# mLSTM cell and squared-ReLU FFN: another order of a step's transfers on the one issuing queue, and weight and block sums moved along VectorE's queue

## The chip, the core and the metric

The kernel runs on one core of one Trainium2 chip. The metric is device time in microseconds (us): the median of the timed runs. A core has a matrix engine (TensorE, PE in the profile, with PEld for its weight loads), VectorE (DVE), ScalarE (ACT), GpSimd (POOL), and a queue of SyncE (SPq) from which nearly all transfers of this kernel are issued, one after the other. The profile is that of one execution.

## The reference, cut to what matters

```python
# attention: batch 4, 8 heads, 768 positions, head size 40
for t in range(S):
    m_new  = np.maximum(f_gate[:, :, t] + m, i_gate[:, :, t])
    f_stab = np.exp(f_gate[:, :, t] + m - m_new)
    i_stab = np.exp(i_gate[:, :, t] - m_new)
    C = f_stab[..., None, None] * C + i_stab[..., None, None] * np.einsum('bhd,bhe->bhde', vt, kt)
    n = f_stab[..., None] * n + i_stab[..., None] * kt
    h_tilde = np.einsum('bhde,bhe->bhd', C, qt)
    denom = np.maximum(np.abs(np.einsum('bhd,bhd->bh', n, qt))[:, :, None], 1.0)
    y[:, :, t] = sigmoid(o_gate[:, :, t]) * h_tilde / denom
# bridge (B,H,S,D) -> (B*S, H*D) = (3072, 320), then
h = np.maximum(x @ w_in, 0.0)          # 320 -> 2048
out = (h * h) @ w_out                  # 2048 -> 320
```

The recurrence is computed in chunks of 128 positions: 24 chunks `s` (6 for each of 4 batch entries). Inside a chunk, the decay between two positions is `exp(A[t] + b[t'])`, where `A` is a running sum of gates for each head; between chunks a state `C` is carried.

## The kernel before: what the change touches

The main loop has *parts* `n`, four to a chunk: `s = 6 + n // 4`, `at = n % 4`. A part holds a quarter of one FFN product of a *group* `g` of two chunks, and beside it one piece of the attention of chunk `s` or `s + 1`. Every engine and the issuing queue work through their own instructions in the order in which the program emits them.

```python
parts = [(1, 2, i) for i in range(4)] + [(2, 0, i) for i in range(4)]
for g in range(1, NG):                                   # NG = 12 groups
    parts += [(2, g, i) for i in range(4)]               # second FFN product of group g: s even
    if g + 2 < NG:
        parts += [(1, g + 2, i) for i in range(4)]       # first FFN product of g + 2 ("fast"): s odd
for n, (which, g, i) in enumerate(parts):
    s, at = 6 + n // 4, n % 4
    ...
    even = s >= 8 and s % 2 == 0
    squares_soon = s >= 7 and s % 2 == 1
    fast = which == 1 and g > 2
    if at == 0:
        if s < 8 or even:
            do(score, s)                   # PE scores; DVE weights them (L458)
        if even:
            do(turn_kq, s + 1)             # DVE 32x32 transposes of the loaded squares (L325)
    if at == 1:
        if even:
            do(lambda s: scores(s, ("h", "h")), s + 1)   # PE, L436: needs turn_kq(s + 1)
        if fast:
            ffn1_rows(g, 0, True)          # PE, L862
        do(attend_turned, s)               # PE numT (L533, L542), dC; DVE transposes tn (L559)
        do(decays, s + 1)                  # ACT exp of the broadcast A (L378)
        do(mask, s + 1)                    # POOL (L368)
        ...
        do(store_num, s)                   # transfer: tn -> DRAM (L571)
        if squares_soon:
            do(load_squares, s + 2)        # 4 transfers of small pieces (L318)
            do(load_num, s)                # 4 transfers: numerators back, turned (L576)
        do(load, s + 4)                    # k and v of s + 4 (L305)
        if 8 <= s < 20:
            load_o(s + 4)                  # L333
        if not squares_soon:
            do(load_num, s)
        do(pair_up, s + 3)                 # 4 transfers DRAM to DRAM (L296)
    ...
    if which == 2 and 0 < g < NG - 1 and i == 3:
        sums(g + 1, slice(0, NPAIR), (2,))               # DVE, block sum S2 (L751)
    if which == 2 and g > 1 and i < 2:
        sums(g, slice(0, NPAIR), (3 + i,))
    if n in (10, 11):
        for more in range(2):
            sums_of_win(2 * (n - 10) + more)             # DVE, sums of w_in (L810, 812, 814, 816)
    ...
    if fast:
        if i % 2:
            ffn1_close(g, i // 2, i == 1)
            ...
        else:
            ffn1_open(g, i // 2)
        ...
    else:
        ffn2_fast(g, i)                    # (for g > 0)
    if at == 2:
        do(lambda s: weigh(s, masked=True), s + 1)       # ACT exp (L392)
        ...
        do(normalise_turned, s)            # DVE, begins at L588: needs load_num(s)
        do(store_rows, s)                  # L623
        if not squares_soon:
            do(load_squares, s + 2)
        do(load_rows, s)                   # L628, needs store_rows(s)
        do(load_A, s + 2)                  # one transfer: A broadcast to all partitions (L343)
```

What the pieces do that matter here:

```python
def load_A(s):                              # two buffers; A[s + 2] takes that of A[s]
    A = ld.tile([P, H, P], F32, name="A_bc", bufs=2)
    nc.sync.dma_start(A[:], bass.AP(A_d.tensor, ..., [[0, P], [S, H], [1, P]]))   # 512 KB

def store_num(s):                           # transposed numerators to DRAM, 256 KB
    nc.sync.dma_start(n_d[s], st[s]["tn"]...)

def load_num(s):                            # read back in another order, 4 x 64 KB
    for m in range(P // SQ):
        nc.sync.dma_start(N[m * SQ : (m + 1) * SQ]..., n_d[s, :, m * P : (m + 1) * P]...)

def load_squares(s):                        # k and q of a chunk as 32x32 squares
    for i in range(2):
        for e in range(0, D, SQ):           # 128 KB in runs of 128 bytes, 32 KB in runs of 32 bytes
            nc.sync.dma_start(t[DP * i + e : ...], kq_d[s, i, ...]...)

def ffn1_open(g, q):                        # first half of a fast first product
    X, Y, V, Z = st["f1"] = [ps_h.tile([P, 4, P], F32, name="h_ps") for _ in range(4)]
    blocks(X, F11, xT[:, 0, 0, :], q, True)          # PE, L830
    nc.scalar.copy(m1[:], X[:])                      # ACT, L843
    blocks(Y, WS[1], xs[:, 3, :], q, True)
    nc.vector.tensor_tensor(U2[:], Y[:], m1[:], op=ALU.add)     # DVE, L845
    blocks(V, WS[0], xs[:, 0, :], q, True)
    nc.vector.tensor_tensor(U4[:], V[:], U2[:], op=ALU.add)     # DVE, L847
    blocks(Z, F22, xs[:, 4, :], q, True)

def ffn1_close(g, q, begun):                # adds on into the same banks
    blocks(X, F12, xT[:, 0, 1, :], q, False)         # PE; X must have been copied (L843)
    ...
    nc.scalar.activation(g4[:, :, 0, t0], X[:], AF.Relu)        # ACT, L878
    tt(U2[:], U2[:], Y[:], op=ALU.add)               # DVE, L879 to L882
    ...
```

`ffn1_rows` adds on into X and Y, so it needs the copy of X (L843) and the addition that reads Y (L845). `sums_of_win` 0 and 1 give `WS[0]` and `WS[1]`; 2 overwrites F21 with F11 − F21; 3 gives `WS[3]` from `WS[1]`.

Of the kernel before, what the change touches and what calls it, by code (L numbers as in the profile page):

```python
# [29 lines left out]
def kernel(  # L30
# [38 lines left out]
    NPAIR = NF // 2  # L69
    GT = 2  # L70
    NG = NT // GT
# [255 lines left out]
    def load_o(s):  # L327
        b, c = divmod(s, NB)
        r, (s0, s1) = next((r, (a, z)) for r, (a, z) in enumerate(RUNS) if a <= s < z)
        if s == s0:  # L330
            st["og", r] = ld.tile([P, 4, H, D], F32, name="og")
        og = st.setdefault(s, {})["og"] = st["og", r][:, s - s0]
        nc.sync.dma_start(og, o_gate[b, :, c * P : (c + 1) * P, :].rearrange("h p d -> p h d"))  # L333
# [314 lines left out]
    def new_g2(g):  # L648
        if g < 2:
            st["g2", g] = ffn.tile([P, NF, WG], F32, name=f"g2_{g}", bufs=1)  # L650
        else:
            st["g2", g] = g2c if g == 2 else st["g2", g - 3]
# [152 lines left out]
    def sums_of_win(i):  # L805
        tt = nc.vector.tensor_tensor
        if i != 2:
            WS[i] = late.tile([P, NPAIR, P], F32, name=f"WS{i}", bufs=1)[:]
        if i == 0:
            tt(WS[0], F21, F22, op=ALU.add)  # L810
        elif i == 1:
            tt(WS[1], WS[0], F11, op=ALU.subtract)
        elif i == 2:
            tt(F21, F11, F21, op=ALU.subtract)
        else:
            tt(WS[3], F12, WS[1], op=ALU.subtract)
# [18 lines left out]
    def ffn1_open(g, q):  # L835
        if q == 0:
            new_g2(g)
        xT, xs = st["xT", g], st["xs"]
        X, Y, V, Z = st["f1"] = [ps_h.tile([P, 4, P], F32, name="h_ps") for _ in range(4)]
        m1, U2, U4 = [ffn.tile([P, 4, P], F32, name="r_sb", bufs=4) for _ in range(3)]  # L840
        st["U"] = U2, U4
        blocks(X, F11, xT[:, 0, 0, :], q, True)
        nc.scalar.copy(m1[:], X[:])  # L843
        blocks(Y, WS[1], xs[:, 3, :], q, True)
        nc.vector.tensor_tensor(U2[:], Y[:], m1[:], op=ALU.add)  # L845
        blocks(V, WS[0], xs[:, 0, :], q, True)
        nc.vector.tensor_tensor(U4[:], V[:], U2[:], op=ALU.add)  # L847
        blocks(Z, F22, xs[:, 4, :], q, True)
# [45 lines left out]
    def do(f, s):  # L894
        if 0 <= s < NT:
            f(s)
# [20 lines left out]
    def load_part(s, i):  # L917
        b, c = divmod(s, NB)
        dst, src = load_parts(s)[i]
        nc.sync.dma_start(dst, src[b, :, c * P : (c + 1) * P, :].rearrange("h p d -> p h d"))  # L920
# [64 lines left out]
    for u in range(8):  # L985
        s = 2 + u // 2
# [70 lines left out]
    for n, (which, g, i) in enumerate(parts):  # L1057
        s, at = 6 + n // 4, n % 4
        if n == 5:
            brought.close()  # L1060
            late = ctx.enter_context(tc.tile_pool(name="late", bufs=1, side="right"))
        even = s >= 8 and s % 2 == 0
        squares_soon = s >= 7 and s % 2 == 1
        fast = which == 1 and g > 2
        if at == 0:
            if s < 8 or even:
                do(score, s)
            if even:
                do(turn_kq, s + 1)
        if at == 1:  # L1070
            if even:
                do(lambda s: scores(s, ("h", "h")), s + 1)
            if fast:
                ffn1_rows(g, 0, True)
            do(attend_turned, s)
            do(decays, s + 1)
            do(mask, s + 1)
            if n > 4 and not even and not fast:
                do(turn_kq, s + 1)
            do(decay_C, s + 1)  # L1080
            if s > X_SQ and not fast:
                do(turn_squares, s - 1)
            do(store_num, s)
            if squares_soon:
                do(load_squares, s + 2)
                do(load_num, s)
            do(load, s + 4)
            if 8 <= s < 20:
                load_o(s + 4)
            if not squares_soon:  # L1090
                do(load_num, s)
            do(pair_up, s + 3)
        if 5 <= n < 8:
            sums_of_weights(n - 5)
        if n == 6:
            sums(1, slice(0, NPAIR), (1, 2))
        if n == 8:
            sums_of_weights(3)
            sums(1, slice(0, NPAIR), (3,))
        if n == 9:  # L1100
            sums(1, slice(0, NPAIR), (4,))
        if which == 2 and 0 < g < NG - 1 and i == 3:
            sums(g + 1, slice(0, NPAIR), (2,))
        if which == 2 and g > 1 and i < 2:
            sums(g, slice(0, NPAIR), (3 + i,))
        if n in (10, 11):
            for more in range(2):
                sums_of_win(2 * (n - 10) + more)
        if at == 3 and s >= 8 and s % 2 == 0 and s // 2 - 1 < NG:
            sums_of_x(s // 2 - 1)  # L1110
        if at == 2 and not fast:
            if n > 4:
                do(scale_q, s + 1)
        if at == 3:
            if s % 4 == 3:
                for r in range(s + 1, min(s + 5, NT)):
                    sigmoid(r)
# [4 lines that stand above are left out]
                    do(turn_kq, s + 1)  # L1122
                    do(turn_squares, s - 1)
            else:
                ffn1_open(g, i // 2)
            if at == 2:
                do(scale_q, s + 1)
        elif which == 1:
            ffn1_main(g, i)
            if i % 2 == 0:  # L1130
                held = st["half"]
            else:

                both = held, st["half"]
                for more, half in enumerate(both):
                    ffn1_rest(g, i - 1 + more, half[0])
                for half in both:
                    st["half"] = half
                    relu_half()
                    square_half()  # L1140
        elif g == 0:
            ffn2(g, *divmod(i, 2))
        else:
            ffn2_fast(g, i)
        if at == 2:
            do(lambda s: weigh(s, masked=True), s + 1)
            ffn1_square()
            if n < 4:
                do(turn_kq, s + 1)
                do(scale_q, s + 1)  # L1150
            if even:
                do(weighted, s + 1)
            do(normalise_turned, s)
            do(store_rows, s)
            if not squares_soon:
                do(load_squares, s + 2)
            do(load_rows, s)
            do(load_A, s + 2)
        if at == 0:
            ffn1_square()  # L1160
        if n < 5:
            while rounding.done < LAST[n]:
                rounding.step()
# [30 lines left out]
```

## Time and profile before

The median of three runs is 521.55 us (518.85 to 525.43). The profiled execution took 521.29 us, of which the profile's span is 519.5 us.

| Engine or queue | busy, us | share of the span |
|---|---|---|
| PE | 498.4 | 96% |
| PEld | 457.9 | 88% |
| VectorE | 339.0 | 65% |
| ScalarE | 248.3 | 48% |
| GpSimd | 109.0 | 21% |

| Transfer (all from SPq) | count | KB each | us to landing, median |
|---|---|---|---|
| A broadcast, `A_bc<-a_rows` | 22 | 512 | 4.7 |
| numerators out, `num_rows<-tn` | 18 | 256 | 3.5 |
| numerators back, `kq<-num_rows` | 72 | 64 | 2.5 |
| squares, `kqT<-kq_rows` | 34 + 34 | 128 and 32 | 3.3 and 3.0 |
| rows out and back, `x_rows`, `xT` | 18 and 72 | 192 and 48 | 2.1 and 2.5 |

How to read the profile's lines: the first two numbers of a timeline line are the start in us from the span's start and the duration in us of what the line merges; then the engine, the source line of the kernel, the operation, what is written and read, and the count. In brackets stands the idle time of that engine just before, and what ended it. A "landing" is the time from a transfer's issue until its completion is signalled. An engine's wait matters only if it makes PE wait, since PE is the busiest.

### The profile page before, as it was taken

The numbers are of one execution on the slowest core, as the hardware profiler recorded it, in microseconds if no ns is written. First come the engines' busy times: TensorE is split into PE (matmuls) and PEld (weight loads), VectorE is DVE, ScalarE is ACT, GpSimd is POOL, SyncE is SP. The second block draws the span as 40 slices with busy tenths as digits, with TensorE's granted clock in tenths as the row PEclk, the third lists the DMA queues.
The fourth block names the chain that finished last, engine by engine and source line by source line (L and its number), as shares of the span: only waits on it lengthen the run. The fifth ranks groups of instructions, "written<-read, shape, count | busy, mean of one in ns | idle before, by whom it ended". The sixth has DMA issues, their size and how long they took to land.

```text
span 519.5 us, 13523 instructions
## 1 busy us (share of the span) xinstructions
PE 498.4 (96%) x5497; PEld 457.9 (88%) x5497; DVE 339.0 (65%) x630; ACT 248.3 (48%) x492; POOL 109.0 (21%) x138
## 2 busy tenths in 40 slices
PE   9989999999998999989999999989899899999997
PEld 4867788787797999989999899979899899999997
DVE  8588966555876866576667766476676676644441
ACT  3768897564440650661642672542482462432500
POOL 3356743321040130112102103103103111020000
PEclk9999999999998999999999999999999999999999
DMA  9999999665645775875765756775754632200000
GB/s 191 226 211 231 234 232 228 104 128 100 163 108 117 146 141 94 169 167 96 165 150 111 162 140 122 147 170 107 160 133 99 137 96 56 80 13 27 1 27 25
DMA packets 238237, 67.73 MB, mean 130 GB/s; under 512 B 185600, under 2 KB 232704, under 8 KB 238176
## 3 DMA queue, kind: packets, MB, share of 16 engines
q1 hardware_dynamic: 238080, 66.68, 61.4%
q8 instruction: 43, 0.70, 0.6%
q10 hardware_dynamic: 96, 0.20, 0.1%
q14 instruction: 18, 0.15, 0.1%
HBM read 54.56 MB, written 17.86 MB: 139 GB/s over the span
## 4 chain that ended last, share of the span: by engine, by line
PE 69%; SPq 8%; DVE 8%; DMA 6%; issue 4%; ACT 3%; POOL 1%; DVEq 0%; POOLq 0%; ACTq 0%
PE h_ps L756 25%; PE h_ps L830 12%; PE h_ps L665 7%; PE h_ps L862 5%; SPq L318 4%; PE h_ps L702 3%; DMA A_bc<-a_rows 3%; PE numT L542 3%; SPq L628 2%; PE h_ps L676 2%; PE hp L481 2%; PE h_ps L436 1%; DVE A_bc L458 1%; PE tp L436 1%; PE idle L909 1%
## 5 line engine op out<-in xcount | busy, mean ns | idle before, releaser
L368 POOL TENSOR_SCALAR_AFFINE_SELECT A_bc<-A_bc 128x1024 f32<-128x1024 f32 x22 | 24.9, 1134 | 223.9 <-ACT kq L378 189.6
L378 ACT ACTIVATE kq<-A_bc 64x512 f32<-64x512 f32 x30 | 18.8, 628 | 80.2 <-DMA A_bc<-a_rows 80.0
L756 PE MATMUL h_ps<-T,S 128*128 128x160 f32 x352 | 51.5, 299 | 0.7 <-DVE g L880 0.7
L756 PEld LDWEIGHTS h_ps<-T,S 128*128 128x128 f32 x352 | 49.0, 190 | 0.9 <-PE h_ps L756 0.9
L392 ACT ACTIVATE A_bc<-A_bc,b_T 128x128 f32<-128x128 f32 x144 | 44.0, 388 | 11.2 <-POOL A_bc L368 10.8
L756 PE MATMUL h_ps<-w_out,g 128*128 128x160 f32 x336 | 49.2, 303 | 0.0
L756 PEld LDWEIGHTS h_ps<-w_out,g 128*128 128x128 f32 x336 | 46.1, 190 | 1.4 <-issue 1.2
L665 PE MATMUL h_ps<-xT,w_in 128*128 128x256 f32 x192 | 44.2, 383 | 2.2 <-ACT xT L644 1.6
L830 PE MATMUL h_ps<-xT,w_in 128*128 128x128 f32 x288 | 39.3, 280 | 4.9 <-ACT r_sb L843 4.9
L665 PEld LDWEIGHTS h_ps<-xT,w_in 128*128 128x128 f32 x192 | 35.5, 190 | 8.1 <-ACT xT L644 2.0
L830 PEld LDWEIGHTS h_ps<-xT,w_in 128*128 128x128 f32 x288 | 35.2, 191 | 6.6 <-ACT r_sb L843 5.7
L772 DVE TENSOR_TENSOR y_sb<-y_sb,h_ps 128x160 f32<-128x160 f32 x44 | 14.0, 318 | 40.7 <-PE h_ps L756 40.6
L559 DVE STREAM_TRANSPOSE tn<-numT 128x256 f32<-128x256 f32 x36 | 16.0, 450 | 37.3 <-PE numT L542 37.3
L862 PE MATMUL h_ps<-xT,w_in 64*64 64x128 f32 x864 | 37.2, 275 | 2.8 <-DVE r_sb L845 2.8
L830 PE MATMUL h_ps<-xs,w_in 128*128 128x128 f32 x288 | 38.0, 275 | 0.0
L843 ACT COPY r_sb<-h_ps 128x512 f32<-128x512 f32 x18 | 10.5, 584 | 55.8 <-PE h_ps L830 55.8
L862 PEld LDWEIGHTS h_ps<-xT,w_in 64*64 64x64 f32 x864 | 32.0, 133 | 5.7 <-DVE r_sb L845 3.5
L830 PE MATMUL h_ps<-xs,WS 128*128 128x128 f32 x288 | 35.1, 275 | 0.0
L830 PEld LDWEIGHTS h_ps<-xs,w_in 128*128 128x128 f32 x288 | 35.1, 192 | 0.0
L830 PEld LDWEIGHTS h_ps<-xs,WS 128*128 128x128 f32 x288 | 33.6, 192 | 0.0
L756 PE MATMUL h_ps<-w_out,g_c 128*128 128x160 f32 x192 | 28.0, 302 | 0.0
L756 PEld LDWEIGHTS h_ps<-w_out,g_c 128*128 128x128 f32 x192 | 26.3, 190 | 0.7 <-issue 0.5
(173 smaller groups left out, 1041.0 us busy)
## 6 DMA issues: line engine op xcount, KB each, us to landing
A_bc<-a_rows SPq DMA_DIRECT2D x22, 512.0 KB, 4.7
raw<-in_moe_w_out_dram SPq DMA_DIRECT2D x8, 640.0 KB, 4.6
num_rows<-tn SPq DMA_DIRECT2D x18, 256.0 KB, 3.5
kq<-num_rows SPq DMA_DIRECT2D x72, 64.0 KB, 2.5
kqT<-kq_rows SPq DMA_DIRECT2D x34, 128.0 KB, 3.3
raw<-in_moe_w_in_dram SPq DMA_DIRECT2D x8, 512.0 KB, 6.0
kq<-in_k_dram SPq DMA_DIRECT2D x24, 160.0 KB, 4.4
va<-in_v_dram SPq DMA_DIRECT2D x24, 160.0 KB, 4.7
```

The lines of the kernel that those rows point to most:

```text
L318: nc.sync.dma_start(t[DP * i + e : DP * i + e + SQ, :, :w], kq_d[s, i, :, :, :, e : e + w].rearrange("n j (m r) a -> r (n j m) a", r=SQ),)
L368: nc.gpsimd.affine_select(A[:], A[:], compare_op=ALU.is_ge, fill=-1e30, base=0, pattern=[[0, H], [1, P]], channel_multiplier=-1,)
L378: nc.scalar.activation(e[rows], st[s]["A"][0][rows, PR * i : PR * (i + 1), :], AF.Exp)
L392: nc.scalar.activation(d["W"][:, i * n + h, :], A[i][:, h, :], AF.Exp, bias=b_T[:, b, c, i * n + h : i * n + h + 1],)
L542: nc.tensor.matmul(numT[i][halves[g], e, :], lhsT=va_w[s % NKQ][:, h * D1 : h * D1 + DP], rhs=d["P"][h % 2][:, h // 2, :] if s < KQ_SQ els ...
L559: nc.vector.transpose(to[:, 2 * i : 2 * i + 2], numT[i][:, :2, :].rearrange("p c t -> p (c t)"))
L665: nc.tensor.matmul(hs[i][:, n, :], lhsT=w_in[:, a, fb * P : (fb + 1) * P], rhs=xT[:, :, a, :], start=(n == 0 and a == 0), stop=False,)
L702: nc.tensor.matmul(o_ps, lhsT=st["g2", g][:, fb, j * P : (j + 1) * P], rhs=w_out[:, fb, :], start=(fb == 0), stop=(fb == NF - 1),)
L756: nc.tensor.matmul(to, lhsT=lhsT[:, p], rhs=rhs[:, p, :], start=(start and p == 0), stop=(p == NPAIR - 1), skip_group_check=True,)
L772: add = lambda to, a, b: nc.vector.tensor_tensor(to, a, b, op=ALU.add)
L830: nc.tensor.matmul(to[:, n, :], lhsT=lhsT[:, 4 * q + n, :], rhs=rhs, start=(start and n == 0), stop=True, skip_group_check=True,)
L862: nc.tensor.matmul(to[cols, n, :], lhsT=w_in2[rows, 4 * q + n, cols], rhs=rhs, start=(start and n == 0), stop=True, skip_group_check=True,)
```

## The change

Four things move; no arithmetic is added or taken away.

1. From chunk 8 on, the broadcast of `A` for chunk `s + 2` is issued right behind the store of the numerators of `s`, at `at == 1`, and no longer at the end of `at == 2`.
2. From chunk 8 on, the order behind that store is the same for all chunks: A, k, the numerators' loads, then (odd chunks) the squares, then v, the o gate and the pairs. Before, odd chunks issued the squares ahead of the numerators' loads, and even chunks k, v and o.
3. The squares of chunk 9, issued at chunk 7, go from `at == 1` to `at == 2`.
4. On VectorE, block sum S2 of group `g + 1` moves from the last part of `ffn2_fast(g)` to the part behind, after the two additions of `ffn1_open`. The four sums of `w_in` move from parts 10, 10, 11, 11 to parts 9, 10, 10, 11.

It is for having the transfers on which engines wait land sooner, and for having the additions that release PE's banks not stand behind long sums on VectorE.

```diff
-        squares_soon = s >= 7 and s % 2 == 1
 ...
             do(store_num, s)
-            if squares_soon:
-                do(load_squares, s + 2)
+            if s >= 8:
+                do(load_A, s + 2)
+                do(lambda s: load_part(s, 0), s + 4)
                 do(load_num, s)
-            do(load, s + 4)
-            if 8 <= s < 20:
-                load_o(s + 4)
-            if not squares_soon:
+                if not even:
+                    do(load_squares, s + 2)
+                do(lambda s: load_part(s, 2), s + 4)
+                if s < 20:
+                    load_o(s + 4)
+            else:
+                do(load, s + 4)
                 do(load_num, s)
             do(pair_up, s + 3)
 ...
-        if which == 2 and 0 < g < NG - 1 and i == 3:
+        if which == 2 and i == 3 and g == NG - 2:
             sums(g + 1, slice(0, NPAIR), (2,))
         if which == 2 and g > 1 and i < 2:
             sums(g, slice(0, NPAIR), (3 + i,))
-        if n in (10, 11):
-            for more in range(2):
-                sums_of_win(2 * (n - 10) + more)
+        for more in {9: (0,), 10: (1, 2), 11: (3,)}.get(n, ()):
+            sums_of_win(more)
 ...
             else:
                 ffn1_open(g, i // 2)
+                if i == 0:
+                    sums(g - 1, slice(0, NPAIR), (2,))
 ...
             do(store_rows, s)
-            if not squares_soon:
+            if s < 8 or even:
                 do(load_squares, s + 2)
             do(load_rows, s)
-            do(load_A, s + 2)
+            if s < 8:
+                do(load_A, s + 2)
```

## The prediction, made before the changed kernel was run

> **What bounds the kernel now.** I read the table of engines first.
>
> ```profile
> PE 498.4 (96%) x5497; PEld 457.9 (88%) x5497; DVE 339.0 (65%) x630; ACT 248.3 (48%) x492; POOL 109.0 (21%) x138
> ```
>
> PE is the bound, and a change that touches no matmul can win back only idle PE time: 519.5 - 498.4 = 21.1 us. So I went through PE's timeline for every idle stretch. From chunk 8 on (about 144 us) there are eleven. The eight that matter:
>
> ```profile
> 163.74 1.12 PE L862 MATMUL h_ps<-xT,w_in 64*64 64x128 f32 x31 [2.43 <-DVE r_sb L845]
> 221.36 2.41 PE L756 MATMUL h_ps<-T,S 128*128 128x160 f32 x16 [0.72 <-DVE g L880]
> 224.86 0.46 PE L436 MATMUL h_ps<-kqT 40*64 40x128 f32 x5 [1.09 <-issue]
> 252.85 1.16 PE L830 MATMUL h_ps<-xT,w_in 128*128 128x128 f32 x8 [0.68 <-ACT r_sb L843]
> 292.85 1.16 PE L830 MATMUL h_ps<-xT,w_in 128*128 128x128 f32 x8 [1.17 <-ACT r_sb L843]
> 343.59 1.22 PE L436 MATMUL h_ps<-kqT 40*64 40x128 f32 x32 [2.50 <-issue]
> 372.48 1.16 PE L830 MATMUL h_ps<-xT,w_in 128*128 128x128 f32 x8 [1.57 <-ACT r_sb L843]
> 411.81 1.16 PE L830 MATMUL h_ps<-xT,w_in 128*128 128x128 f32 x8 [1.50 <-ACT r_sb L843]
> ```
>
> With three more (0.17 at 263.29, 0.21 at 281.49, 0.16 at 321.20) they make 12.20 us. The other 8.9 us lie where the change does nothing: 0.93 at the start, 4.96 in six gaps up to 97 us, 3.03 after PE's last product (516.47). The gaps have three causes.
>
> *First, late A.* The timeline of chunk 19, all engines, around the gap at 372.48:
>
> ```profile
> 365.56 0.42 SPq L343 DMA_DIRECT2D A_bc<-a_rows  x1
> 370.06 1.27 ACT L378 ACTIVATE kq<-A_bc 64x512 f32<-64x512 f32 x2 [11.34 <-DMA A_bc<-a_rows]
> 371.84 0.58 ACT L843 COPY r_sb<-h_ps 128x512 f32<-128x512 f32 x1
> ```
>
> ScalarE stands 11.34 us at `decays` for A; behind it queues the copy of X that lets PE go on. A was issued at 365.56 at the end of a queue. Chunks 13, 15, 19, 21 show this: 0.68 + 1.17 + 1.57 + 1.50 = 4.92 us.
>
> *Second, late numerators.* Chunk 17, around 343.59, where the page gives only "issue":
>
> ```profile
> 326.99 0.38 SPq L571 DMA_DIRECT2D num_rows<-tn  x1
> 327.43 4.69 SPq L318 DMA_DIRECT2D kqT<-kq_rows  x4
> 332.21 3.12 SPq L576 DMA_DIRECT2D kq<-num_rows  x4
> 336.95 0.17 DVE L588 TENSOR_SCALAR dm<-kq 128x8 f32<-128x8 f32 x1 [4.83 <-DMA kq<-num_rows]
> 342.25 1.23 DVE L325 STREAM_TRANSPOSE kqT<-kqT 128x1024 f32<-128x1024 f32 x1
> ```
>
> VectorE waits 4.83 us for numerators issued behind 4.69 us of squares; normalising, four additions, weighting and the transposes of the next squares follow in order, and PE's scores start at 343.59, just after that transpose ends (343.48). These gaps: 0.72 + 1.09 + 0.17 + 2.50 = 4.48 us.
>
> *Third, VectorE's queue ahead of the first opening:*
>
> ```profile
> 159.37 1.22 DVE L751 TENSOR_TENSOR S<-S,g_c 128x1024 f32<-128x1024 f32 x1
> 160.50 1.22 DVE L814 TENSOR_TENSOR w_in<-w_in 128x1024 f32<-128x1024 f32 x1
> 161.64 1.22 DVE L816 TENSOR_TENSOR WS<-w_in,WS 128x1024 f32<-128x1024 f32 x1
> 163.01 0.68 DVE L845 TENSOR_TENSOR r_sb<-h_ps,r_sb 128x512 f32<-128x512 f32 x1
> ```
>
> L845 ends at 163.69 and L862 starts at 163.74: 2.43 us, with 0.37 us more of the kind in chunks 15 and 17. It also cost clock. A table of stages, columns stretch, length, busy us (instructions) of PE, PEld, DVE, ACT and POOL, granted clock, DMA share, GB/s:
>
> ```profile
> 165.00:169.00 4.00, 4.00 (x75) 3.65 (x67) 0.61 (x2) 0.00 (x0) 0.00 (x0) 0.57 0.80 198
> ```
>
> 4.00 x (1 - 0.57) = 1.72 us.
>
> [...] 0.57 followed the 2.43 us gap, but the stage 340 to 350 us, with the gap of 2.50, kept 1.00. [...] `load_num` cannot follow its store at once. In chunk 18 the store was issued at 346.36, the load at 349.76. [...] Between the stores of chunks 17 and 19 (39.7 us) the issues here add up to 30.8 us[...].
>
> **The change part by part.**
>
> *A sooner.* For A of even chunks (the late ones) the issue goes from the end of one even chunk's queue to just behind its store: A of chunk 20 from 365.56 to just after the store at 346.36, 18.8 us earlier. Its landing (4.7 us) is then long past when `decays` comes. Its buffer, that of chunk 18, has been read by then, since the store itself waits for the same numT products. The 4.92 us go.
>
> *But they hide something.* From chunk 17 I take an allowance. Its numT products end at 324.64 (323.61 + 1.02). PE is ready for the next scores when L756 ends, 341.09 (338.75 + 2.34), or 16.45 later. From L588's start to the transpose's end VectorE needs 343.48 - 336.95 = 6.53. So L588 may start 9.9 us after numT without loss. It started 12.3 after: 2.4 predicted, 2.50 seen. Chunk 11: 218.23 - 206.29 = 11.9, or 2.0, against 0.72 + 1.09. For chunks 13, 15, 19, 21 the same distance is 11.2, 10.8, 11.4, 11.1: they would lose 1.3 + 0.9 + 1.5 + 1.2 = 4.9 us if A did not already hold PE that long. A alone would gain nearly nothing; the numerators must come 1 to 2.4 us sooner as well.
>
> *Numerators sooner.* After the change: the store goes out about 1.8 us after numT (now 2.35 in chunk 17, with A's 0.42 and its handover ahead). It lands in about 3.2 (median 3.5; 4.7 in chunk 17, where A went just ahead): 5.0. Four issues of 0.47: 6.9. The last lands 1.7 to 2.5 later: 8.6 to 9.4, inside 9.9. A and k now lie ahead[...], so I keep 0.3 us a chunk for six chunks: 1.8 us. The 4.48 go less that.
>
> *Squares behind.* Issued from about 6.9 to 9.7 (four of about 0.65, or 4.7[...]: 11.6), landing 3.3 later, 13 to 15. The transpose needs them at 9.9 + 6.53 - 1.23 = 15.2. Just enough.
>
> *Chunk 9's squares.* They move behind the rows' store (135.25), so issue 135.7 to 138.4 and landing about 141.5. Their transpose ran at 140.05 to 141.28, PE wants it by 143.20: 142.7, no gap, small margin. I keep 0.4 us.
>
> *Sums.* Part 9 takes L810 (1.22) into an idle VectorE stretch (2.10 us before 150.65); part 10 has L814 in its place; part 11 loses S2 and L814, 2.4 us. So L845 ends near 161.5 with PE ready at 161.3: 0.25 of the 2.43 stay. The clock's 1.72 come back. S2 then runs where VectorE waits for numT (2.3 to 3.7 us in those chunks), costs nothing, and the 0.37 go.
>
> Sum: 4.92 + 4.48 + 2.43 + 0.37 + 1.72 = 13.9; less 1.8 + 0.4 + 0.25 = 11.5 us. I take 0.7 off for an issuing queue that gets fuller relative to a shorter span: 10.8, 521.6 - 10.8 = 510.8 us.
>
> **Rivals.**
> - *The numerators stay the bound*: A's 512 KB and k's many short pieces delay them[...] as the squares did. For: stores issued right behind A (266.67, 306.56) had their loads only 4.6 and 4.9 us later. Against: now the store goes first. Then only the third cause and some of the second go: 4 to 6 us, 516.
> - *The issuing queue becomes the bound*: in odd chunks it now idles about 2 us for the store to land, which squares used to fill. For: 30.8 of 39.7. Against: even chunks have slack (numerators landed about 2 us before L588). Squares would be late, gaps before L436 stay at about 1 us: 514 to 515.
> - *Everything lands in time*: 13.9 less 0.5, 508.
>
> **Range and chances.** A 2% gain is 10.4 us, 511.1. My centre lies just under; misses lie rather above, since PE has at most 13.9 to give. Loss over 2% would need a new wait in every chunk. Range 506.8 to 517. Faster by over 2%: 0.51; within: 0.47; slower: 0.02.
>
> **What would show it.** Right: PE busy near 497, ScalarE's wait for A gone (80.0 us now), no gap at L830 behind L843 after chunk 9, the clock 1.00 in the stage around 165 us, L588 starting less than 10 us after numT in odd chunks. Wrong: gaps before L436 still over 1 us in odd chunks, L588 waiting as long for numerators, L325 waiting for squares, or a new gap at 143 us.

## The result and the profile after

The changed kernel takes **506.39 us** (median of 4 runs, 504.20 to 507.42). The kernel before, run beside it, takes 523.16 us (median of 4). The ratio is **0.968** (95% interval 0.961 to 0.976), a gain of 3.2%. Predicted were 510.8 us with a range of 506.8 to 517.0: the direction was right, the gain was larger, and the median lies 0.4 us below the range.

The engines' table of the kernel after, and the row of the granted clock in 40 slices:

```profile
PE 497.2 (99%) x5497; PEld 458.8 (91%) x5497; DVE 342.4 (68%) x630; ACT 248.1 (49%) x492; POOL 116.8 (23%) x138
...
PEclk9997999999999999999999999999999999999999
```

PE's busy time is what it was (498.4), in a span shorter by 15.2 us. From 99 us to its last product at 501.28 PE has no idle gap at all; before it had eleven from chunk 8 on. (Idle times under 0.15 us are not listed; from chunk 8 on there are none of those either.) The 7 in the clock row is a drop near 40 us, where the change does nothing; the profiled run of before had none there.

The part of the timeline of after that answers to the one shown of chunk 17 (numT ends at 314.64 + 1.09 = 315.73); issuing queue, VectorE and PE:

```profile
316.98 0.38 SPq L571 DMA_DIRECT2D num_rows<-tn  x1
317.52 0.37 SPq L343 DMA_DIRECT2D A_bc<-a_rows  x1
317.94 0.70 SPq L920 DMA_DIRECT2D kq<-in_k_dram  x1
319.32 2.10 SPq L576 DMA_DIRECT2D kq<-num_rows  x4
321.46 3.58 SPq L318 DMA_DIRECT2D kqT<-kq_rows  x4
325.04 0.17 DVE L588 TENSOR_SCALAR dm<-kq 128x8 f32<-128x8 f32 x1 [1.82 <-DMA kq<-num_rows]
330.35 1.24 DVE L325 STREAM_TRANSPOSE kqT<-kqT 128x1024 f32<-128x1024 f32 x1
332.12 1.10 PE L436 MATMUL h_ps<-kqT 40*64 40x128 f32 x32
```

The numerators' loads go out 3.6 us after numT, L588 starts 9.3 after it, inside the allowance of 9.9, and the scores at L436 start with no bracket: no idle time before them. L588 still waits 1.82 us, but the transposes that follow it end at 331.59, before PE is ready for the scores.

The list of waits (waiter, what it waited for, us in total, times, longest), two lines of ScalarE's and one of VectorE's; first of before:

```profile
ACT kq L378 <- DMA A_bc<-a_rows: 80.0, 13, 11.6
...
DVE dm L588 <- DMA kq<-num_rows: 15.9, 7, 4.8
...
ACT L378 <- DMA A_bc<-a_rows: 1.9, 1, 1.9
```

and of after:

```profile
ACT L378 <- DMA A_bc<-a_rows: 3.8, 1, 3.8
...
ACT kq L378 <- DMA A_bc<-a_rows: 1.4, 1, 1.4
...
DVE dm L588 <- DMA kq<-num_rows: 8.6, 7, 2.3
```

ScalarE's 81.9 us of waiting for A have shrunk to 5.2, VectorE's for numerators from 15.9 to 8.6. Three landings moved; the page's list of transfers, the last column being us from issue to landing:

```profile
A_bc<-a_rows SPq DMA_DIRECT2D x22, 512.0 KB, 5.3
num_rows<-tn SPq DMA_DIRECT2D x18, 256.0 KB, 2.4
kq<-num_rows SPq DMA_DIRECT2D x72, 64.0 KB, 3.4
```

The store lands in 2.4 us (3.5 before), the loads behind it in 3.4 (2.5), A in 5.3 (4.7).

At the first opening of chunk 9, the third cause of idle time:

```profile
160.67 1.22 DVE L816 TENSOR_TENSOR WS<-w_in,WS 128x1024 f32<-128x1024 f32 x1
161.81 0.32 DVE L772 TENSOR_TENSOR y_sb<-y_sb,h_ps 128x160 f32<-128x160 f32 x1
162.04 0.69 DVE L845 TENSOR_TENSOR r_sb<-h_ps,r_sb 128x512 f32<-128x512 f32 x1
162.41 1.48 PE L862 MATMUL h_ps<-xT,w_in 64*64 64x128 f32 x33
163.44 1.22 DVE L751 TENSOR_TENSOR S<-S,g_c 128x1024 f32<-128x1024 f32 x1
```

Block sum S2 (L751) now runs behind L845, and PE enters L862 without a gap.

**Where the time went.** I set the starts of the numT products (L542) of both kernels side by side. At chunk 8 the kernel after is still 1.78 us *late*: it lost 3.41 us to the early clock drop (granted clock 0.50 from 40.5 to 47.3 us) and won part back in shorter early gaps (1.8 us less). From chunk 8 on it gains only:

```
chunk   before    after   gained    PE's idle time before, in that stretch
  9     166.98   165.12     3.64    2.43 (163.74) and clock 1.72
 10     186.96   184.37     0.73    (rest of the clock's loss)
 12     226.01   221.20     2.22    0.72 + 1.09
 14     264.88   258.77     1.30    0.68 + 0.17
 15     283.83   277.08     0.64    0.21
 16     304.52   296.33     1.44    1.17
 17     323.54   314.64     0.71    0.16
 18     344.74   333.16     2.68    2.50
 20     384.15   370.73     1.84    1.57
 22     423.48   408.29     1.77    1.50
```

The chunks left out gained 0.00. From the start of chunk 8's numT to PE's last product, which I call **the stretch** from here on, it is 371.80 us before (144.67 to 516.47) and 354.83 after (146.45 to 501.28): 16.97 us less. Of these 12.20 are the idle gaps and 1.72 the clock. The other **3.05 us** are in no gap: the rows gain a little more than their idle time, 3.05 / 11 = 0.28 us a gap on average.

### The profile page after: what moved, and what is told of

Read it like the earlier page. It is cut to its first block, busy times and chain, and to the rows that moved or that the text cites. A ratio compares the mean times of both kernels' runs of the same rounds, so it can differ in the third digit from the quotient of the medians.

```text
span 504.3 us, 13521 instructions
## 1 busy us (share of the span) xinstructions
PE 497.2 (99%) x5497; PEld 458.8 (91%) x5497; DVE 342.4 (68%) x630; ACT 248.1 (49%) x492; POOL 116.8 (23%) x138
## 4 chain that ended last, share of the span: by engine, by line
PE 96%; DVE 1%; ACT 1%; issue 0%; DVEq 0%
PE h_ps L756 34%; PE h_ps L830 23%; PE h_ps L665 8%; PE h_ps L862 7%; PE numT L542 4%; PE h_ps L702 3%; PE hp L481 2%; PE h_ps L676 2%; PE h_ps L436 2%; PE tp L436 2%; PE idle L909 1%; PE numT L533 1%; PE tp L421 1%; PE tp L444 1%; PE dC L474 1%; PE dC L552 1%
## 5 line engine op out<-in xcount | busy, mean ns | idle before, releaser
L756 PE MATMUL h_ps<-T,S 128*128 128x160 f32 x352 | 51.4, 299 | 0.0
L843 ACT COPY r_sb<-h_ps 128x512 f32<-128x512 f32 x18 | 10.5, 585 | 79.0 <-PE h_ps L830 79.0
L756 PE MATMUL h_ps<-w_out,g 128*128 128x160 f32 x336 | 49.2, 303 | 0.0
L756 PEld LDWEIGHTS h_ps<-T,S 128*128 128x128 f32 x352 | 49.0, 190 | 0.0
L756 PEld LDWEIGHTS h_ps<-w_out,g 128*128 128x128 f32 x336 | 46.1, 190 | 1.4 <-issue 1.2
L830 PE MATMUL h_ps<-xT,w_in 128*128 128x128 f32 x288 | 38.9, 278 | 0.0
L830 PE MATMUL h_ps<-xs,w_in 128*128 128x128 f32 x288 | 38.0, 275 | 0.0
L830 PEld LDWEIGHTS h_ps<-xT,w_in 128*128 128x128 f32 x288 | 35.2, 192 | 0.9 <-issue 0.7
L862 PE MATMUL h_ps<-xT,w_in 64*64 64x128 f32 x864 | 35.8, 273 | 0.0
L404 POOL TENSOR_TENSOR vw<-va,A_bc 128x328 f32<-128x328 f32 x15 | 13.7, 915 | 93.4 <-issue 48.1
L830 PE MATMUL h_ps<-xs,WS 128*128 128x128 f32 x288 | 35.1, 275 | 0.0
L830 PEld LDWEIGHTS h_ps<-xs,w_in 128*128 128x128 f32 x288 | 35.1, 192 | 0.0
L830 PEld LDWEIGHTS h_ps<-xs,WS 128*128 128x128 f32 x288 | 33.6, 192 | 0.0
L862 PEld LDWEIGHTS h_ps<-xT,w_in 64*64 64x64 f32 x864 | 31.3, 133 | 2.3 <-DVE r_sb L845 0.2
L756 PE MATMUL h_ps<-w_out,g_c 128*128 128x160 f32 x192 | 28.0, 302 | 0.0
L756 PEld LDWEIGHTS h_ps<-w_out,g_c 128*128 128x128 f32 x192 | 26.3, 190 | 0.7 <-issue 0.5
```

What stands on the lines that cost most here:

```text
L404: nc.gpsimd.tensor_tensor(d["vw"][:], d["va"][:], d["W"][:, :, P - 1 : P].to_broadcast([P, H, D1]), op=ALU.mult,)
L756: nc.tensor.matmul(to, lhsT=lhsT[:, p], rhs=rhs[:, p, :], start=(start and p == 0), stop=(p == NPAIR - 1), skip_group_check=True,)
L830: nc.tensor.matmul(to[:, n, :], lhsT=lhsT[:, 4 * q + n, :], rhs=rhs, start=(start and n == 0), stop=True, skip_group_check=True,)
L862: nc.tensor.matmul(to[cols, n, :], lhsT=w_in2[rows, 4 * q + n, cols], rhs=rhs, start=(start and n == 0), stop=True, skip_group_check=True,)
```

## The experiments

In the profiles the part ahead of chunk 8 loses 0 to 5 us to the clock, mostly near 40 us but anywhere from 14 to 74 us, so each run is read by its stretch, with PE's idle gaps in it and the clock's loss in it, and by its ratio to the kernel before, run beside it. A stretch is that of one execution: the kernel after gave 354.83 and 355.24 in two, and the granted clocks of repeated executions differ (0.980 to 0.997 for the kernel before), so a clock drop of 1.7 us can be there in one and not in the next. A table of all, in us:

| Run | median | ratio [interval] | stretch | idle (gaps) | clock | rest |
|---|---|---|---|---|---|---|
| before | | 1 | 371.80 | 12.20 (11) | 1.72 | 357.88 |
| after | 506.39 | 0.968 [0.961, 0.976] | 354.83 | 0 (0) | 0 | 354.83 |
| a_alone | 529.25 | 1.013 [1.006, 1.020] | 371.30 | 10.84 (9) | 3.40 | 357.06 |
| num_alone | 529.43 | 1.009 [1.005, 1.014] | 376.43 | 13.70 (15) | 1.70 | 361.03 |
| sums_alone | 523.75 | 0.999 [0.997, 1.002] | 374.23 | 13.40 (11) | 3.44 | 357.39 |
| transfers_only | 511.46 | 0.977 [0.972, 0.981] | 359.75 | 3.12 (1) | 1.72 | 354.91 |
| no_a | 533.36 | 1.012, one execution each | 380.75 | 19.23 (15) | 1.70 | 359.82 |
| no_num_order | 531.66 | 1.009, one execution each | 378.65 | 15.74 (10) | 6.80 | 356.11 |
| stalls | 518.52 | 0.984, one execution each | 364.40 | 6.05 (5) | 1.72 | 356.63 |
| after_again | 507.18 | 0.967 [0.963, 0.971] | 355.24 | 0.23 (1) | 0 | 355.01 |
| weigh_first | 508.53 | 0.969 [0.966, 0.972] | 355.69 | 0.66 (1) | 0 | 355.03 |
| a_ahead_of_store | 528.88 | 1.010 [1.007, 1.013] | 375.93 | 14.21 (9) | 5.12 | 356.60 |
| a_behind_numerators | 515.12 | 0.982 [0.977, 0.987] | 364.90 | 5.96 (3) | 3.42 | 355.52 |
| early_fill | 506.05 | 0.967 [0.964, 0.970] | 354.82 | 0 (0) | 0 | 354.82 |

"Rest" is the stretch less idle and clock.

### A alone

To the kernel before, only A's new place.

```diff
             do(store_num, s)
+            if s >= 8:
+                do(load_A, s + 2)
             if squares_soon:
                 do(load_squares, s + 2)
 ...
-            do(load_A, s + 2)
+            if s < 8:
+                do(load_A, s + 2)
```

> The kernel before with one thing changed: from chunk 8 on A for chunk s + 2 is issued right behind the numerators' store. Measured by the stretch from the numT products (L542) of chunk 8 to the end of PE's last product: 371.8 us before, 354.8 after the whole change. Theory (late A and late numerators hide each other): the four gaps behind L843 go, but gaps before L436 of about 1 us or more open in chunks 13, 15, 19 and 21 besides those of 11 and 17; stretch 369 to 375, no gain. Rival (the causes add up): the four gaps go and nothing comes, stretch 365.8.

Stretch 371.30 against 371.80: A alone gains nothing, as the prediction said. (The timed runs are even 1.3% slower; three of the four had a granted clock of 0.974 to 0.980, the profiled one 0.987.) All gaps behind the copy of X (L843) are gone; in the same chunks PE now waits at the scores behind. PE's timeline of this kernel at the scores of chunk 14, where before had 0.68 at L830 and only 0.17 here:

```profile
270.23 1.11 PE L436 MATMUL h_ps<-kqT 40*64 40x128 f32 x29 [2.07 <-issue]
```

The squares are still ahead of the numerators (store 252.75, A 253.22, four squares 253.68 to 258.32, numerators 258.43), so L588 starts 12.0 us after the numT of chunk 13 (251.39), and what that costs was hidden before behind the wait for A.

### The numerators' order alone

To the kernel before, the new order behind the store, with A left at the end.

```diff
-            if squares_soon:
+            if s == 7:
                 do(load_squares, s + 2)
                 do(load_num, s)
+                do(load, s + 4)
+            elif s >= 8:
+                do(lambda s: load_part(s, 0), s + 4)
+                do(load_num, s)
+                if not even:
+                    do(load_squares, s + 2)
+                do(lambda s: load_part(s, 2), s + 4)
 ...
```

> The kernel before with the order of the loads alone: k, numerators' loads, then squares, v, o; A stays at the end of at == 2. Theory and the rival of adding up agree here: the gaps at L436 and L756 in chunks 11, 13 and 17 (4.48 us of idle time) go, with some 0.3 us more for each that PE needs to get going again: stretch 366.0; the four gaps behind L843 stay at 1 to 1.6 us. If the numerators were bound by their store's landing and not by the squares ahead of them: stretch over 369.

A miss: stretch 376.43, slower by 4.6 us, where a gain was expected. The issuing queue of this kernel, chunk 17:

```profile
331.25 0.42 SPq L343 DMA_DIRECT2D A_bc<-a_rows  x1
...
332.39 0.38 SPq L571 DMA_DIRECT2D num_rows<-tn  x1
332.82 0.48 SPq L920 DMA_DIRECT2D kq<-in_k_dram  x1
336.91 1.74 SPq L576 DMA_DIRECT2D kq<-num_rows  x4
338.70 4.05 SPq L318 DMA_DIRECT2D kqT<-kq_rows  x4
```

Here A goes out right *ahead* of the store. The store lands only 4.5 us after its issue, and the queue stands from 333.30 to 336.91 doing nothing, since everything behind is held back by the loads' wait. Taking the squares out of this wait left a hole in the queue: in odd chunks from 11 to 19 the numerators' loads went out 6.4 to 7.1 us after numT (6.6 to 7.6 before), hardly earlier, and all that follows, A of the next chunk included, came later. Of the two branches of the expectation it is the second, the store's landing, that came true; that A ahead of the store is what delays the landing is tested below.

### The sums alone

```diff
-        if which == 2 and 0 < g < NG - 1 and i == 3:
+        if which == 2 and i == 3 and g == NG - 2:
             sums(g + 1, slice(0, NPAIR), (2,))
 ...
-        if n in (10, 11):
-            for more in range(2):
-                sums_of_win(2 * (n - 10) + more)
+        for more in {9: (0,), 10: (1, 2), 11: (3,)}.get(n, ()):
+            sums_of_win(more)
 ...
                 ffn1_open(g, i // 2)
+                if i == 0:
+                    sums(g - 1, slice(0, NPAIR), (2,))
```

> The kernel before with VectorE's moves alone (S2 behind the opening, sums of w_in sooner). Theory: the gap of 2.43 at the first opening and the clock's 1.72 behind it go, and the gaps of 0.21 and 0.16; stretch 366.4, all other gaps stay. If the clock's drop comes at a random place and not from that gap: a stage with a clock near 0.5 stays somewhere behind 150 us, stretch 368.

A miss: ratio 0.999 [0.997, 1.002], no difference; the one stretch is 2.4 us longer, 1.2 of it idle time and 1.7 clock. The gap of 2.43 shrank to 0.17, and this appeared 11 us behind it, where before had none:

```profile
174.78 1.16 PE L830 MATMUL h_ps<-xT,w_in 128*128 128x128 f32 x8 [1.36 <-ACT r_sb L843]
```

PE came sooner and met the late A, for which ScalarE waits 11.71 us here, until 172.36. The idle time and the clock's loss moved to later gaps; the transfers set the pace.

### All transfers, no sums

The kernel after with the sums of before.

```diff
-        if which == 2 and i == 3 and g == NG - 2:
+        if which == 2 and 0 < g < NG - 1 and i == 3:
             sums(g + 1, slice(0, NPAIR), (2,))
 ...
-        for more in {9: (0,), 10: (1, 2), 11: (3,)}.get(n, ()):
-            sums_of_win(more)
+        if n in (10, 11):
+            for more in range(2):
+                sums_of_win(2 * (n - 10) + more)
 ...
-                if i == 0:
-                    sums(g - 1, slice(0, NPAIR), (2,))
```

> The changed kernel without VectorE's moves: A and the loads' order as after, S2 and the sums of w_in as before. Theory: only the gap at the first opening (2.4 us, with the clock's drop) and small ones before L862 are left; stretch 360.2, that is 5.4 more than after. With a_alone at 0 and num_alone at -5.6 the pair would be worth -11.6: far more than the sum of both alone. Rival (adding up): the same time here, but then a_alone must have given 6.

As expected: 359.75, with one gap left.

```profile
165.52 1.22 PE L862 MATMUL h_ps<-xT,w_in 64*64 64x128 f32 x31 [3.12 <-DVE r_sb L845]
```

So the two moves of transfers, -0.5 and +4.6 alone, are worth -12.05 together; and the sums, +2.4 on top of before, are worth 359.75 - 354.83 = 4.9 on top of the transfers: 3.12 idle, 1.72 clock, 0.08 rest.

### After without A's move

```diff
             if s >= 8:
-                do(load_A, s + 2)
                 do(lambda s: load_part(s, 0), s + 4)
 ...
-            if s < 8:
-                do(load_A, s + 2)
+            do(load_A, s + 2)
```

(chunk 9's squares go back to part `at == 1` with it)

> The changed kernel with A back at the end of at == 2. Theory: the four gaps behind L843 are back (4.9 us of idle time, about 1.1 more for four restarts), nothing else; stretch from chunk 8's numT to PE's end 360.8 (354.8 after, 371.8 before).

A miss: 380.75, the slowest stretch of all, 26 us above after. It is the numerators' order alone with the sums: the queue again stands before L576 (A 312.33, store 312.84, loads 317.77), and A comes so late that there are gaps of 2.57, 2.73, 2.40 and 2.88 behind L843.

### After with the squares ahead of the numerators

```diff
             if s >= 8:
                 do(load_A, s + 2)
-                do(lambda s: load_part(s, 0), s + 4)
+            if squares_soon:
+                do(load_squares, s + 2)
                 do(load_num, s)
-                if not even:
-                    do(load_squares, s + 2)
-                do(lambda s: load_part(s, 2), s + 4)
-                if s < 20:
-                    load_o(s + 4)
-            else:
-                do(load, s + 4)
+            do(load, s + 4)
+            if 8 <= s < 20:
+                load_o(s + 4)
+            if not squares_soon:
                 do(load_num, s)
```

(chunk 9's squares go back to part `at == 1` with it)

> The changed kernel with the old order of the other loads (odd chunks: squares ahead of the numerators; A ahead of both). Theory: gaps before L436 in all odd chunks from 11 to 21, 1 to 3 us each; stretch 364 to 370. Rival (adding up): 354.8 + 5.6 = 360.4.

Slower than expected: 378.65. Behind A the squares took 5.49 us to issue in chunk 17 (331.62 to 337.11), the loads went out 8.2 us after numT, L588 came 13.4 after it, and PE waited:

```profile
349.00 1.22 PE L436 MATMUL h_ps<-kqT 40*64 40x128 f32 x32 [3.56 <-issue]
```

Three gaps (2.23, 3.56, 3.03) cost clock besides, 6.80 us.

### Stalls put in on purpose

To measure what a stall costs beyond its idle time: the kernel after, computing S2 again 2, 3, 2 and 3 times ahead of four openings (the same values; only time is added).

```diff
             else:
+                if i == 0:
+                    for _ in range({5: 2, 6: 3, 7: 2, 8: 3}.get(g, 0)):
+                        sums(g - 1, slice(0, NPAIR), (2,))
                 ffn1_open(g, i // 2)
```

> The changed kernel, with block sum S2 computed 2, 3, 2, 3 extra times on VectorE ahead of the openings of groups 5, 6, 7, 8 (same values written again). Each puts a stall of about 1.1, 2.3, 1.1, 2.3 us before L862 in a place that has none. It measures what a stall costs: the shift of everything behind it against the idle time that the profile shows. Theory: each shift is the idle time plus about 0.3 us; where the clock drops behind it, 1.7 us more. Rival: the shift is the idle time alone, and the 3 us that the change gave beyond its idle time came from somewhere else.

The four gaps, and one more of 0.27 at 186.10:

```profile
241.34 1.12 PE L862 MATMUL h_ps<-xT,w_in 64*64 64x128 f32 x31 [0.43 <-DVE r_sb L845]
...
281.79 1.99 PE L862 MATMUL h_ps<-xT,w_in 64*64 64x128 f32 x32 [2.46 <-DVE r_sb L845]
...
321.84 1.12 PE L862 MATMUL h_ps<-xT,w_in 64*64 64x128 f32 x31 [0.43 <-DVE r_sb L845]
...
361.55 1.11 PE L862 MATMUL h_ps<-xT,w_in 64*64 64x128 f32 x31 [2.46 <-DVE r_sb L845]
```

The stretch grew by 364.40 - 354.83 = 9.57: 6.05 idle, 1.72 clock, and 1.80 in no gap, 0.36 a gap. The rival, that idle time is all, falls. The two gaps of 2.46 differ in what followed; a table of stages, the clock in the third column from the end:

```profile
282.00:286.00 4.00, 4.00 (x82) 3.83 (x80) 1.66 (x2) 0.00 (x0) 0.00 (x0) 0.60 0.35 79
362.00:366.00 4.00, 4.00 (x109) 3.78 (x102) 2.82 (x6) 0.00 (x0) 0.00 (x0) 1.00 0.34 78
```

Equal gaps, and only one lost the clock. What sets them apart was not shown.

### The early clock drop

The kernel after once more, beside a version that weights chunk 2 before a rounding step of the weights, to close the 1.1 us gap at 39 us ahead of the drop:

```diff
                 scores(s)
-                rounding.step()
 ...
             weighted(s)
+            if u == 0:
+                rounding.step()
```

> The changed kernel once more, to have it beside the next kernel on one chip and to see whether its clock drop at 40 to 48 us comes again: it followed a gap of 1.26 us at 39.69 us. If the drop is bound to that gap it is in this profile too[...]. Ratio to before 0.968.

> The changed kernel, and in addition the scores of chunk 2 are weighted (L458) on VectorE before a step of the weights' rounding, not behind it. Theory: the gap of 1.26 us before dC at 39.69 us shrinks to 0.3 or less, and with it the reason for a clock drop there; 1.2 us sooner than after_again, up to 4.5 in executions where that one drops. Rival: the rounding comes 1.3 us later instead and PE waits for w_in at L665 as long as it waited here: no difference.

After repeats itself: 0.967. weigh_first gains nothing: that gap closed, but PE then waited 2.27 us at 46.19 and 1.17 at 67.14, and lost 1.70 us of clock at 70. A third try fills the early gaps with ten products on zeros into a bank that nothing reads:

```diff
+    def fill(n):
+        t = ps_o.tile([P, W], F32, name="tp", tag="o_ps")
+        for _ in range(n):
+            nc.tensor.matmul(t[:], lhsT=zeros..., rhs=zeros..., start=True, stop=True)
 ...
+    fill(2)
     weigh(2, masked=True)
 ...
+                if u == 4:
+                    fill(4)
                 turn_rows(s - 1)
 ...
+            if u == 1:
+                fill(4)
             attend(s)
```

> The changed kernel, with dummy bf16 matmuls (0.22 us each, into an unused bank) where PE stands idle in the early part: 2 behind the turn of chunk 1's rows, 4 ahead of dC of chunk 2, 4 ahead of the turn of chunk 3's rows. All profiles but that of before lost 1.7 to 5.1 us to a clock of about 0.5 in the first 75 us, behind such gaps. Theory: with the gaps filled PE's clock stays up, chunk 8's numT starts at 143 to 145 us (145.9 and 146.5 after), and the time is 1.5 to 3.5 us less. Rival: the drops have another cause, the dummies only shift things: no difference, or slower by their 0.5 us.

The clock row of this kernel:

```profile
PEclk9999999999999999999999999999999999999999
```

The drop is gone, but chunk 8's numT starts at 145.17 against 145.87 and 146.45 in the two profiles of after: up to 1.3 us, and the ratio, 0.967 [0.964, 0.970], can't be told from that of after. The profiled run of before, without the drop too, is there at 144.67. So of the 3.41 us of clock lost at 40 us some 1 to 2 reach chunk 8. In a_alone and stalls, whose drop lies at 67 us, chunk 8's numT starts only at 149.4 and 149.3; whether the place of the drop makes that difference was not tested.

### A ahead of the store

One swap of two issues in the kernel after:

```diff
-            do(store_num, s)
             if s >= 8:
                 do(load_A, s + 2)
+            do(store_num, s)
+            if s >= 8:
                 do(lambda s: load_part(s, 0), s + 4)
```

> The changed kernel with one swap: from chunk 8 on A is issued right ahead of the numerators' store, not right behind it. Theory now: what made the numerators come sooner is that A's 512 KB no longer lie ahead of their store. Then the store lands in about 4.5 us (2.6 after, 4.3 before), the numerators' loads go out near 5.9 us after numT (4.2 after), L588 starts 10.5 to 11.5 us after numT in odd chunks, over the allowance of 9.9, and gaps of 0.5 to 1.5 us open before L436: stretch from chunk 8's numT to PE's end 360 to 364 (354.8 after). Rival: A only has to be early and the squares behind the numerators, whatever the place of the store: stretch under 356.

The direction was right, the size was far off: 375.93, 21 us more than after. The list of the queue's waits, first of after:

```profile
SPq L576 <- DMA num_rows<-tn: 17.9, 18, 1.6
SPq L628 <- DMA x_rows<-x_sb: 15.4, 9, 1.8
```

and of this kernel, with its transfers' landings:

```profile
SPq L576 <- DMA num_rows<-tn: 59.2, 18, 4.7
SPq L628 <- DMA x_rows<-x_sb: 15.4, 9, 1.9
```

```profile
num_rows<-tn SPq DMA_DIRECT2D x18, 256.0 KB, 4.8
kq<-num_rows SPq DMA_DIRECT2D x72, 64.0 KB, 2.0
```

The store lands in 4.8 instead of 2.4 us, and the queue waits 59.2 - 17.9 = 41.3 us longer in 18 stores, 2.3 a store. In odd chunks from 11 to 19 the numerators' loads go out 6.7 to 9.5 us after numT (3.6 to 5.0 in after).

### A behind the numerators

```diff
             if s >= 8:
-                do(load_A, s + 2)
                 do(lambda s: load_part(s, 0), s + 4)
                 do(load_num, s)
+                do(load_A, s + 2)
                 if not even:
                     do(load_squares, s + 2)
```

> The changed kernel with A issued behind the numerators' loads, ahead of the squares. Theory: A is still 8 us or more early; the numerators' data no longer lie behind A, so their loads land in 2.0 to 2.7 us (3.6 after) and L588 starts 7.5 to 8.5 us after numT in odd chunks; but PE has no gap left that this could close: stretch 354.8 to 355.5, same time as after. Rival: A ahead of the squares delays these, L325 waits for them and gaps open before L436: stretch over 357.

A miss: 364.90, 10 us above after. A is behind the store, but ahead of the squares, whose small pieces then take longer to issue. Issuing queue and PE of this kernel in chunk 17 (numT ends at 322.58):

```profile
326.66 0.38 SPq L571 DMA_DIRECT2D num_rows<-tn  x1
327.09 0.45 SPq L920 DMA_DIRECT2D kq<-in_k_dram  x1
329.22 1.74 SPq L576 DMA_DIRECT2D kq<-num_rows  x4
331.13 0.38 SPq L343 DMA_DIRECT2D A_bc<-a_rows  x1
331.55 5.12 SPq L318 DMA_DIRECT2D kqT<-kq_rows  x4
...
341.27 1.95 PE L436 MATMUL h_ps<-kqT 40*64 40x128 f32 x32 [2.24 <-issue]
```

The squares take 5.12 us to issue (3.58 in after), and the queue stands 1.68 us before L576 with nothing to fill the wait. The rows' transfers slip into the next chunk, so its store goes out 4.1 us after numT instead of 1.2: L588 starts at +12.1 in chunks 13 and 17, where the gaps of 2.56 and 2.24 lie. In chunk 11 L588 starts at +8.7, but L325 waits 2.19 us for squares, which makes the third gap, 1.16. Chunks 15 and 19 have none.

### What the runs say together

Take a pair of chunks (four pairs, from the store of chunk 11 to that of 19) and add what the issuing queue can't avoid by itself: time spent issuing, and its waits for its own stores to land (L576, L628). In us a pair:

| Kernel | issuing | L576 | L628 | sum | period |
|---|---|---|---|---|---|
| after | 31.07 | 1.96 | 1.82 | 34.9 | 37.31 |
| transfers_only | 31.19 | 1.81 | 1.81 | 34.8 | 37.27 |
| before | 32.16 | 0.38 | 1.84 | 34.4 | 39.64 |
| a_alone | 33.53 | under 0.13 | 1.81 | 35.3 | 39.55 |
| no_num_order | 33.56 | under 0.13 | 1.85 | 35.4 | 40.92 |
| num_alone | 28.38 | 7.46 | 1.77 | 37.6 | 40.61 |
| no_a | 28.82 | 7.54 | 1.85 | 38.2 | 41.21 |
| a_ahead_of_store | 28.36 | 7.99 | 1.86 | 38.2 | 39.98 |
| a_behind_numerators | 31.47 | 3.18 | 3.37 | 38.0 | 39.76 |

PE without gaps needs 37.3 a pair. There are two ways to be slower. In the last four rows the queue alone needs more than PE: its wait for the store stands empty and is long, or A slows down what is behind it. In before, a_alone and no_num_order the wait is filled, but with the squares, so the numerators are late. With A behind the store and the squares behind the numerators the wait is short, for two reasons that the table separates: from a_ahead_of_store to a_behind_numerators A's 512 KB no longer lie ahead of the store, and L576 falls from 7.99 to 3.18; from there to after, A is issued inside the wait, where it takes 0.37 us to issue and nobody needs it soon, and L576 falls to 1.96. That is why the moves don't add: each removes what hid the other's cost. That the queue is a bound in the last four is read from this table; no run made its issues cheaper, so it isn't shown by itself.

## Why the prediction was right and wrong

**Right in mechanism.** The three causes were the ones, and all eleven gaps are gone (after_again has one of 0.23). "*But they hide something*" held: A alone gained 0.5 us of stretch ("nearly nothing"). "*Numerators sooner*" held: L588 was foreseen at 8.6 to 9.4 us after numT, with 9.9 allowed; it came at 8.5 to 9.8 in odd chunks from 11 to 21, in chunk 15 with only 0.1 us to spare; that this number came out is in part luck, since two errors in it cancel (below). "*Squares behind*": the transpose starts at +14.6 in chunk 17, before the 15.2. "*Chunk 9's squares*": L325 waited 0.85 us there, ended at 144.00, and the scores started at 144.97 with no gap. "*Sums*": the gap and the clock's 1.72 are won back.

**The rivals.** "Everything lands in time" was the one that happened. "The numerators stay the bound" fell, by the landing of the store. "The issuing queue becomes the bound" fell for this change (34.9 of 37.3), and is what four of the experiments ran into, as far as the table tells. The idle time before L576 was foreseen at about 2 us in odd chunks; 0.7 to 1.4 was found in those from 11 to 19, 1.96 a pair. The prediction's figure for this rival was the issues alone (30.8 of 39.7 us). They do not show it, if the queue is the bound in no_a: 28.82 of 41.21 us there are issues, and the rest are waits.

**The step that failed** is the sentence "PE has at most 13.9 to give", and with it the reserves. In the stretch 16.97 us came, 6.2 more than the 10.8 predicted, of two parts:

- *The sum of idle and clock isn't a ceiling.* 12.20 + 1.72 = 13.92 was right as a sum, but a stall cost PE more than its gap: 3.05 us in eleven gaps. The run with stalls put in shows it the other way round (1.80 in five). Over all twelve kernels of the table that have gaps, the rests above 354.83 sum to 25.0 us in 91 gaps, 0.28 a gap, with 0.08 to 0.41 for single kernels. The spread has an order. The traces of these stretches have the same 4480 products of PE, so their starts can be set beside those of after, one by one. Where no clock drop disturbs, the delay across a gap was the gap and a fixed amount more, whatever the gap's length (0.15 to 3.1 us): 0.26 to 0.27 us where L830 or L756 starts again, 0.42 for L862 (0.06 in chunk 9), 0.10 for L436. In before these amounts make 2.5 of the 3.05; the other 0.5 is not assigned. For L830 it can be read off the starts around the gap of 1.57 in before: the last product ahead starts at 370.63, the first behind at 372.48, the second at 372.69, while without a gap they start 0.11 apart. That is 1.84 us of delay, the 1.84 of chunk 20 in the table above. Of the 0.26 beyond the gap, 0.16 is lost overlap (a product's record lasts 0.28 us, so it reaches over the next starts), and 0.10 is a slower first product (its record lasts 0.38).
- *The reserves weren't needed.* 1.8 us for numerators behind A, 0.4 for chunk 9's squares, 0.25 left at L862, 0.7 for the queue: 3.15 in all, and nothing of it came. For the 1.8 the reason was measured. I took 3.2 us for the store's landing, from a median in which A had often been issued just ahead of it. It lands in 2.4, and the loads behind A in 3.4 instead of "1.7 to 2.5": the two errors nearly cancel, which is luck.

3.05 + 3.15 = 6.2. Against this, the profiled run of after came to chunk 8 1.78 us later. The timed medians differ by 16.8 and the profiled spans by 15.2. That fits the clocks on record: 0.997 in the profiled run of before, which had no early drop, and 0.980 to 0.993 in 43 of the 44 runs of that kernel beside the experiments.

The range failed at its low end for the same reason: it was built with "misses lie rather above", on the belief in a ceiling.

**What I would also have got wrong.** Before the runs I took sums and numerators to be worth 5 us each alone. They are worth nothing, or less, alone. The prediction of the whole held only because the whole was changed.

## What to carry to other kernels

Keep large transfers from lying just ahead of a store whose landing is waited for. Between that store and the load that reads it back is the place for a large transfer that is cheap to issue and not needed soon: the same transfer just ahead of the store, or behind the load and just ahead of small-piece transfers, cost 21 and 10 us of stretch here. For an issuing queue like the one here, compare its issuing time plus its waits for its own landings with the bound engine's time per period, and judge moves on such a queue together, since each may hide another's cost. When counting PE's idle gaps, add 0.1 to 0.4 us a gap (0.28 on average here), also for the shortest ones (0.15 us here), and for long ones the risk of clock: here 16 of the 22 gaps of 2.07 to 3.56 us were followed by a drop that cost about 1.7 us or twice that.

## What I had not expected of the hardware

- The landing of the numerators' store (256 KB) doubled, from 2.4 to 4.8 us (medians of 18), when the broadcast of A (512 KB) was issued right ahead of it on the same queue. It is the swap of one pair of issues that shows it (a_ahead_of_store against after).
- The squares, transfers of small pieces, took longer to *issue* right behind the broadcast. The four squares of odd chunks 11 to 19, issued 0.4 to 0.5 us behind A, took 5.1 to 6.1 us (a_behind_numerators), 4.5 to 5.8 (no_num_order) and 4.4 to 4.6 (a_alone); in after, with the numerators' loads between, 2.8 to 3.6.
- The clock. Of 17 gaps of 2.07 to 2.88 us in the stretches of all kernels, 11 were followed by a drop of the granted clock to 0.50; of 5 gaps of 3.03 to 3.56 us, all. Of 5 gaps of 1.75 to 1.96 us, one was. Each drop cost about 1.7 us, that is half clock for 3.41 us (in before from 165.08 to 168.49), or twice that. The length of a gap alone does not decide: of the two of 2.46 in stalls only the first was followed by a drop (0.60 in the 4 us behind it, 1.00 behind the second), and in before the one of 2.43 was (0.57 from 165 to 169), that of 2.50 was not (1.00 from 340 to 350). Ahead of chunk 8 shorter gaps went either way: behind 1.26 us at 39.69 in after the clock was 0.50 from 40.5 to 47.3; behind 1.05 us at 99.22 in after and 1.18 at 64.87 in before it stayed at 1.00. What else decides was not shown.
